# Gates of eight pairs loaded one token per partition, with a new order table and 123 fill-in matmuls

## The chip, the cores and the metric

The kernel runs on one NeuronCore of a Trainium2 chip. The core has a matrix engine (TensorE, PE in the profile, with its weight loads as PEld), a vector engine (VectorE, DVE), a scalar engine (ScalarE, ACT), a general engine (GpSimd, POOL) and a sync engine (SyncE, SP) that does nothing but start transfers. Transfers between the chip's memory and the core's on-chip memory run on 16 DMA engines, which all queues share. Each compute engine works through its own list of instructions in order; semaphores make it wait for others. The metric is the device time of one execution in microseconds, as the median of several runs.

## What is computed

The reference has two stages, all in float32. The inputs q, k, v and the gates a_re, a_im have the shape 4 x 8 x 768 x 48 (batch, head, token, feature).

The first stage is a recurrence over the tokens with a complex gate, in each batch and head:

```python
mag = np.sqrt(a_re * a_re + a_im * a_im)
scale = np.minimum(mag, 0.999) / (mag + 1e-06)
a_re_n, a_im_n = (a_re * scale, a_im * scale)
for t in range(S):
    new_re = ar * S_re - ai * S_im
    new_im = ar * S_im + ai * S_re
    S_re, S_im = (new_re + kv, new_im)        # kv: outer product of k[t], v[t]
    y[:, :, t] = np.einsum('bhd,bhde->bhe', q[:, :, t], S_re)
```

The second takes y as 4 x 768 rows of 384 features and applies a normalisation and an MLP with a residual:

```python
xn = (x - mu) / np.sqrt(var + 1e-06) * g_ln
ch = np.maximum(xn @ w_ch1, 0.0) @ w_ch2      # 384 -> 1536 -> 384
out = x + ch
```

## The kernel before

**Tiling.** The 768 tokens of a batch are six chunks of 128, taken two at a time: twelve pairs of chunks (P = 0 to 11, three per batch), 24 chunks (n = 0 to 23). Eight heads of 48 features lie side by side as 384 columns.

**From gates to a matrix product.** In logarithms the product of the gates up to a token is a cumulative sum. For each pair the kernel loads both gates (`are`, `aim`, 384 KB each, line 445), takes the log of the real part (`ln`), its inverse (`iv`), the ratio `r` = a_im / a_re, and from it the log magnitude (`r2`, `u`, `l`, `lc`) and the angle (`th`). Two groups of matmuls with a triangle of ones sum them over the tokens: `dec` (line 477, log magnitude) and `ph` (lines 492 to 496, angle in turns, with a carry `car` from the pair before). ACT then makes the decay `e`, its inverse `en`, and sine and cosine. q and k are multiplied by these (`qe`, `ke`, then `qs`, `ks`), transposed (`qT`, `kT` on PE with a copy out, or by a transposing DMA, line 599), and give a causal 128 x 128 score matrix per head (`am`, masked into `atm`). `gm` and `G` carry the state from chunk to chunk, `y` is the output of the recurrence, copied to `x`.

**The MLP.** x is transposed (`xtr`, `xT`), and each pair runs through 1536 hidden features in three groups: `mm1` (line 722), `relu` (lines 739 and 741, on ACT or DVE), `mm2` (line 754). Mean and scale of the normalisation are folded into the weights (`wp`, `wc`) and into the output scale `rstd`; `oa`, `ot` and `st` scale, add the residual and store (line 777).

**How tokens lie in the gate tiles.** For the gates alone partition p of a pair holds the two neighbouring tokens 2p and 2p + 1, so that one run in memory is 2 x 48 numbers, 384 B. q, k and v hold token p of each chunk, in runs of 192 B. The two cumulative sums turn the one arrangement into the other: for each of the two chunks c they add the products with two triangles `u_e[:, c, j]` (or `u_th`), j being the first or second token of a partition:

```python
for c in range(R):
    for j in range(R):
        nc.tensor.matmul(heads(ps[:, c]), lhsT=u_e[:, c, j], rhs=step(T("l", P), j),
                         start=(j == 0), stop=(j == R - 1))
```

That is four matmuls of 384 columns per pair and sum.

**The order of the work.** Nothing is scheduled on the chip. A table, `PLAN`, written out in full, holds all operations in one sequence, each with its engine (P, A, V, G, S for PE, ACT, DVE, POOL, SP) and, where it uses the accumulator memory, its bank. Every engine gets its operations in that sequence. For a load or a store the letter says which queue starts it, SP's or ACT's; a DMA that ACT starts stands in ACT's list with its arithmetic. `@name` makes an operation of POOL wait for the named one of DVE. Buffers are rings (line 26): three for the gates, q and k, two for v's load, four to five for what leaves.

**Fill-ins.** 134 matmuls without use (`warm`, line 787) stand among the work of the head and keep PE busy while the first gates are loaded and worked on.

Of the kernel before, what the change touches and what calls it, by code (L numbers as in the profile page):

```python
# [10 lines left out]
FP16 = mybir.dt.float16  # L11
# [23 lines left out]

ENGINES = {"P": "PE", "A": "ACT", "V": "DVE", "G": "POOL", "S": "SP"}
# [3 lines left out]
aim.0.0:A tab.log.0:A aim.0.1:A ue:G are.0.0:S are.0.1:S pad.e.1:G uth:V one:G warm.0:P0 pad.ks.0:G warm.1:P0  # L40
warm.2:P0 pick:G warm.3:P0 are.1.0:S warm.4:P0 warm.5:P0 warm.6:P0 k.0.1:S ln.0.0:A warm.7:P0 car0.1:G warm.8:P0
cmean:G iv.0.0:A warm.9:P0 ident:G warm.10:P0 warm.11:P0 r.0.0:V warm.12:P0 warm.13:P0 warm.14:P0 aim.1.0:S warm.15:P0
warm.16:P0 warm.17:P0 ln.0.1:A warm.18:P0 warm.19:P0 r2.0.0:A warm.20:P0 k.0.0:S warm.21:P0 warm.22:P0 warm.23:P0
warm.24:P0 u.0.0:A warm.25:P0 warm.26:P0 warm.27:P0 warm.28:P0 iv.0.1:A warm.29:P0 l.0.0:V warm.30:P0 are.2.0:S
warm.31:P0 warm.32:P0 ln.1.0:A warm.33:P0 warm.34:P0 r.0.1:G warm.35:P0 lc.0.0:V warm.36:P0 warm.37:P0 aim.2.0:S
warm.38:P0 warm.39:P0 warm.40:P0 iv.1.0:A warm.41:P0 warm.42:P0 pad.ks.1:G warm.43:P0 warm.44:P0 warm.45:P0 warm.46:P0
warm.47:P0 zdec:G r2.0.1:A warm.48:P0 pad.e.0:G warm.49:P0 pad.qs.0:G warm.50:P0 q.0.1:S warm.51:P0 warm.52:P0 u.0.1:A
warm.53:P0 warm.54:P0 r.1.0:V warm.55:P0 dec.0.0:P0 warm.56:P1 warm.57:P1 q.1.0:S e.0.0:A0 warm.58:P1 warm.59:P1
warm.60:P1 r2.1.0:V warm.61:P1 en.0.0:A0 warm.62:P1 warm.63:P1 warm.64:P1 l.0.1:V warm.65:P1 u.1.0:A warm.66:P1
warm.67:P1 warm.68:P1 warm.69:P1 lc.0.1:V warm.70:P1 are.3.0:S warm.71:P1 warm.72:P1 warm.73:P1 ln.2.0:A warm.74:P1  # L50
l.1.0:V warm.75:P1 warm.76:P1 warm.77:P1 warm.78:P1 dec.0.1:P6 q.1.1:S warm.79:P0 warm.80:P0 lc.1.0:V en.0.1:A6
warm.81:P0 warm.82:P0 warm.83:P0 warm.84:P0 q.0.0:S iv.2.0:A warm.85:P0 warm.86:P0 ke.0.1.0:G@lc.1.0 warm.87:P0
dec.1.0:P0 e.0.1:A6 r.2.0:V wl.1:G warm.88:P2 warm.89:P2 e.1.0:A0 warm.90:P2 warm.91:P2 warm.92:P2 warm.93:P2
warm.94:P2 gln:S r2.2.0:V en.1.0:A0 qrow:G dps.1:P4 dps.0:P5 ke.0.0.0:V warm.95:P2 warm.96:P2 u.2.0:A warm.97:P2
warm.98:P2 decc.1:V4 warm.99:P2 vf.0.0:S car0.0:G warm.100:P2 warm.101:P2 warm.102:P2 mask:G warm.103:P2 warm.104:P2
aim.3.0:S tab.trig.1:A warm.105:P2 warm.106:P2 warm.107:P2 wl.0:G qe.1.0.1:V warm.108:P2 warm.109:P2 vf.0.1:S
warm.110:P2 warm.111:P2 warm.112:P2 qe.1.0.0:V warm.113:P2 warm.114:P2 pad.qs.1:G warm.115:P2 warm.116:P2 l.2.0:V
th.0.0:A warm.117:P2 warm.118:P2 wl.2:G warm.119:P2 ph.0.0:P1 th.0.1:A th.1.0:A qe.0.0.0:V ph.0.1:P4 qe.0.1.0:V
warm.120:P0 warm.121:P0 warm.122:P0 k.1.0:S car.0.0:V1 decc.0:V5 sin.0.0:A1 lc.2.0:V sin.0.1:A4 qt.0.0:P1 ks.0.0.1:V
warm.123:P0 car.0.1:A4 wgc:V cos.0.0:A1 qt.0.1:P4 ph.1.0:P6 k.1.1:S ks.0.1.1:V cos.0.1:A4 qs.0.1.1:V th.2.0:A  # L60
# [153 lines left out]
def kernel(  # L214
# [14 lines left out]
    C = 128  # L229
# [594 lines left out]
```

## Time and profile before

| | us |
|---|---|
| median of 3 runs (lowest, highest) | 190.85 (190.52, 192.0) |
| the profiled execution | 192.75 |
| its span, first to last instruction | 191.0 |
| PE busy (2045 matmuls) | 177.3 |
| ACT busy | 158.9 |
| DVE busy | 156.6 |
| POOL busy | 105.5 |

The profile is of one execution. Busy time counts arithmetic: starting a transfer isn't counted, but while a queue engine does so it can do nothing else, and the profile shows such instructions as SPq and ACTq with a duration of their own. A matmul's duration is from its start to its modelled end; matmuls overlap, so the sum of durations is more than the time they take, and the chain of waits gives the step from one to the next. In the DMA rows a share of 1 means that the durations of all packets add up to 16 engines' time; packets overlap, so it can go above 1.

### The profile page before, as it was taken

The numbers are of one execution on the slowest core, as the hardware profiler recorded it, in microseconds if no ns is written. First come the engines' busy times: TensorE is split into PE (matmuls) and PEld (weight loads), VectorE is DVE, ScalarE is ACT, GpSimd is POOL, SyncE is SP. The second block draws the span as 40 slices with busy tenths as digits, with TensorE's granted clock in tenths as the row PEclk, the third lists the DMA queues.
The fourth block names the chain that finished last, engine by engine and source line by source line (L and its number), as shares of the span: only waits on it lengthen the run. The fifth ranks groups of instructions, "written<-read, shape, count | busy, mean of one in ns | idle before, by whom it ended". The sixth has DMA issues, their size and how long they took to land.

```text
span 191.0 us, 5154 instructions
## 1 busy us (share of the span) xinstructions
PE 177.3 (93%) x2045; PEld 138.6 (73%) x2045; DVE 156.6 (82%) x285; ACT 158.9 (83%) x224; POOL 105.5 (55%) x124
## 2 busy tenths in 40 slices
PE   5999398999999999999968999999999999998992
PEld 3888365788667887776847687877867777786781
DVE  1678699999999999999996998998989867666532
ACT  3989499999999997899949999998999979662340
POOL 7419032579196899071539483347785954940130
PEclk9999999999999999999999999999999999999998
DMA  6999999999969999889999999999799979994032
GB/s 153 278 240 202 212 198 204 210 214 207 242 108 287 205 220 234 154 183 234 136 265 234 190 221 230 282 223 204 141 160 262 217 126 179 256 191 151 5 124 82
DMA packets 133080, 37.57 MB, mean 197 GB/s; under 512 B 127168, under 2 KB 133056, under 8 KB 133056
## 3 DMA queue, kind: packets, MB, share of 16 engines
q1 hardware_dynamic: 107760, 27.21, 70.6%
q10 hardware_dynamic: 22512, 7.67, 18.0%
q0 software_dynamic: 2784, 2.36, 7.9%
q8 instruction: 16, 0.26, 0.6%
q14 instruction: 8, 0.07, 0.1%
HBM read 28.31 MB, written 4.72 MB: 173 GB/s over the span
## 4 chain that ended last, share of the span: by engine, by line
PE 63%; DVE 10%; ACT 9%; DMA 8%; issue 4%; ACTq 2%; POOL 1%; SPq 1%; DVEq 0%; POOLq 0%
PE banks L754 22%; PE banks L722 16%; PE banks L617 5%; PE banks L594 4%; DMA q<-in_q_dram 4%; DMA ksT<-ks 3%; PE banks L477 3%; PE banks L667 2%; ACTq L777 2%; PE banks L496 2%; PE banks L670 2%; DVE w1b L388 2%; DMA are<-in_a_re_dram 2%; PE banks L645 2%; PE banks L688 2%
## 5 line engine op out<-in xcount | busy, mean ns | idle before, releaser
L754 PE MATMUL banks<-w2b,h 128*128 128x384 bf16 (+1 forms) x300 | 55.7, 319 | 0.6 <-ACT h L739 0.6
L722 PE MATMUL banks<-xT,w1b 128*128 128x256 bf16 x432 | 50.9, 272 | 0.7 <-ACT h L739 0.5
L722 PEld LDWEIGHTS <-w1b 128*128 128x128 bf16 x432 | 41.4, 98 | 7.0 <-issue 1.2
L754 PEld LDWEIGHTS <-h 128*128 128x128 bf16 x300 | 26.7, 97 | 13.8 <-ACT h L739 1.0
L295 DVE TENSOR_TENSOR atm<-banks,mask 128x1024 bf16<-128x1024 f32 x24 | 29.0, 1219 | 3.8 <-PE banks L617 2.9
L739 ACT ACTIVATE h<-banks 128x1024 bf16<-128x1024 f32 (+1 forms) x26 | 25.7, 1009 | 4.6 <-DVE ks L295 2.6
L792 ACT ACT_TABLE_LOAD x19 | 24.4, 1283 | 2.6 <-PEq L808 1.3
L295 POOL TENSOR_TENSOR ke<-k,en 128x384 bf16<-128x384 f32 x17 | 15.4, 916 | 14.1 <-ACT e L481 4.3
L767 POOL TENSOR_TENSOR ot<-ot,x 128x384 f32<-128x384 f32 x13 | 12.5, 967 | 14.2 <-ACT ot L760 12.9
L295 POOL TENSOR_TENSOR r<-aim,are 128x768 f16<-128x768 f32 (+1 forms) x8 | 13.7, 1715 | 11.0 <-DVE w1b L388 4.1
L787 PE MATMUL banks<-u_e 128*128 128x256 f16 x134 | 17.5, 286 | 2.2 <-POOL u_e L323 2.2
L295 POOL TENSOR_TENSOR qs<-qe,trig 128x768 bf16<-128x768 bf16 x8 | 13.0, 1640 | 10.3 <-DVE w1b L388 7.2
L617 PE MATMUL banks<-qsT,ksT 128*128 128x128 bf16 x192 | 14.5, 219 | 2.8 <-ACT h L739 2.1
L787 PEld LDWEIGHTS <-u_e 128*128 128x128 f16 x134 | 13.5, 102 | 4.5 <-POOL u_e L323 1.9
L617 PEld LDWEIGHTS <-ksT 128*128 128x128 bf16 x192 | 12.1, 97 | 5.1 <-issue 2.8
L741 DVE TENSOR_SCALAR h<-banks 128x1024 bf16<-128x1024 f32 (+1 forms) x11 | 12.7, 1166 | 2.7 <-PE banks L722 2.7
L295 POOL TENSOR_TENSOR qe<-q,e 128x384 bf16<-128x384 f32 x12 | 11.0, 917 | 6.8 <-DVE r L295 3.6
L466 DVE SCALAR_TENSOR_TENSOR l<-r,w 128x768 f16<-128x768 f16 (+1 forms) x13 | 12.6, 969 | 1.3 <-ACT r L462 1.1
L680 DVE BATCH_NORM_STATS2 stats<-x 128x6 f32<-128x384 bf16 x24 | 13.1, 546 | 0.1
L667 PE MATMUL banks<-v,atm 128*128 128x48 bf16 x192 | 12.0, 183 | 0.0
L514 ACT ACTIVATE trig<-banks 128x768 bf16<-128x768 int16 (+1 forms) x13 | 9.8, 761 | 2.5 <-DVE car L509 2.4
L496 PE MATMUL banks<-th,u_th 128*128 128x384 f16 (+1 forms) x52 | 11.8, 313 | 0.0
(93 smaller groups left out, 380.8 us busy)
## 6 DMA issues: line engine op xcount, KB each, us to landing
k<-in_k_dram SPq DMA_DIRECT2D x24, 192.0 KB, 5.1
q<-in_q_dram SPq DMA_DIRECT2D x24, 192.0 KB, 4.3
are<-in_a_re_dram SPq DMA_DIRECT2D x11, 384.0 KB, 5.1
aim<-in_a_im_dram SPq DMA_DIRECT2D x11, 384.0 KB, 5.0
out_dram<-ot ACTq DMA_DIRECT2D x19, 192.0 KB, 3.4
vf<-in_v_dram ACTq DMA_DIRECT2D x18, 192.0 KB, 4.3
w1b<-in_moe_w_ch_dram POOLq DMA_DIRECT2D x3, 384.0 KB, 7.6
vf<-in_v_dram SPq DMA_DIRECT2D x6, 192.0 KB, 7.0
```

The source lines that it names most:

```text
L295: {"DVE": nc.vector, "POOL": nc.gpsimd}[eng(name)].tensor_tensor(**kw)
L466: nc.vector.scalar_tensor_tensor(out=S_("l"), in0=S_("r2"), scalar=0.5, in1=S_("w"), op0=ALU.mult, op1=ALU.add)
L496: nc.tensor.matmul(heads(ps[:, c]), lhsT=u_th[:, c, j], rhs=step(T("th", P), j), start=False, stop=(j == R - 1), skip_group_check=True)
L617: nc.tensor.matmul(ps[:, h], lhsT=T("ksT", n)[:, h], rhs=T("qsT", n)[:, h], start=True, stop=True)
L667: nc.tensor.matmul(ps[:, h], lhsT=T("atm", n)[:, h], rhs=T("v", P)[:, c, h], start=True, stop=nfirst)
L680: nc.vector.bn_stats(out=T("stats", n), in_=T("x", n))
L722: nc.tensor.matmul(ps[:, jj], lhsT=w1b[:, dc, ts(gi * JG + jj, C)], rhs=T("xT", P)[:, dc].rearrange("p c t -> p (c t)"), start=(dc == 0), ...
L739: act(out=dst, in_=src, func=AF.Relu)
L741: nc.vector.tensor_scalar(out=dst, in0=src, scalar1=0.0, scalar2=None, op0=ALU.max)
L754: nc.tensor.matmul(bank(own)[:, 0:w], lhsT=T("h", P)[:, j, ts(c, C)], rhs=w2b[:, j, es], start=(j == 0), stop=(j == NJ - 1))
L787: g.add(f"warm.{i}", lambda i=i: nc.tensor.matmul(bank(f"warm.{i}")[:, 0:256], lhsT=u_e[:, 0, 0], rhs=u_e[:, 1].rearrange("p j t -> p (j t ...
L792: g.add(f"tab.{nm}.{i}", lambda tab=tab: nc.scalar.preload_act_table_set(tab))
```

## The change

Three things change at once.

For the pairs 4 to 11 (`NATURAL`) the gates lie like q, k and v: token p of chunk c. Each gate is loaded as two transfers of 192 KB, one per chunk, in runs of 192 B (operations `are.P.0.c`, `aim.P.0.c`). The logarithms and the angle work on the same 768 columns as before. In the cumulative sums chunk 0 is one product with a triangle, and chunk 1 one with a block of ones (for chunk 0's tokens) and one with the triangle: three matmuls instead of four in `dec`, and three beside the two of the carry in `ph`. Two small tables, `n_e` and `n_th`, hold triangle and ones.

The order table is new from end to end, and its sequence of DMA issues is laid out for eight transfers under way at a time. Counted over both tables: SP starts 130 transfers (before 110) and ACT 38 (39). On ACT there are now 20 loads of q, k and the real gate's parts that SP started before, and 5 of v (18), 11 stores (19). Transposes by DMA: 13 of ks, 12 of qs, 3 of x (before 14, 11, 0). The arithmetic moves a little between engines; ACT, for one, has 1 square (4), 2 conversions of v (4), 15 copies of x (12), 27 ReLUs (26). POOL has 38 waits for its turn (27).

Fill-ins: 123 instead of 134. They stand in blocks of ten to forty, where the old table strewed them.

The code, without the table:

```diff
+NATURAL = {4, 5, 6, 7, 8, 9, 10, 11}
...
+    n_th = pool.tile([C, R, C], FP16, name="n_th")
+    n_e = pool.tile([C, R, C], FP16, name="n_e")
...
+    def c_ne():
+        nc.gpsimd.memset(n_e, 1.0)
+        nc.gpsimd.affine_select(out=n_e[:, 0], in_=n_e[:, 0], pattern=[[1, C]],
+                                compare_op=ALU.is_ge, fill=0.0, base=0, channel_multiplier=-1)
+
+    def c_nth():
+        nc.vector.tensor_scalar(out=n_th, in0=n_e, scalar1=INV2PI, scalar2=None, op0=ALU.mult)
...
-            def step(t, j, hs=hs):
+            nat = P in NATURAL
+
+            def step(t, j, hs=hs, nat=nat):
+                if nat:
+                    return t.rearrange("p h x -> p (h x)")[:, ds(j * DM, DM)].rearrange(
+                        "p (h d) -> p h d", d=D)
                 return t[:, hs].rearrange("p h (j d) -> p h j d", j=R)[:, :, j]
+
+            def sums(c, step_t, nat_t, nat=nat):
+                if nat:
+                    return [(nat_t[:, 0 if j == c else 1], j) for j in range(c + 1)]
+                return [(step_t[:, c, j], j) for j in range(R)]
...
+                if nat:
+                    for c in range(R):
+                        add(f"{nm}.{X}.{c}", lambda nm=nm, ap=ap, X=X, c=c, step=step: ring(
+                            f"{nm}.{X}.{c}").dma_start(out=step(T(nm, P), c), in_=ap[b].rearrange(
+                                "h (c p) d -> p c h d", p=C)[:, pp * R + c]), uses=[(nm, P)])
...
                 for c in range(R):
-                    for j in range(R):
-                        nc.tensor.matmul(heads(ps[:, c]), lhsT=u_e[:, c, j], rhs=step(T("l", P), j),
-                                         start=(j == 0), stop=(j == R - 1))
+                    parts = sums(c, u_e, n_e)
+                    for i, (lhsT, j) in enumerate(parts):
+                        nc.tensor.matmul(heads(ps[:, c]), lhsT=lhsT, rhs=step(T("l", P), j),
+                                         start=(i == 0), stop=(i == len(parts) - 1))
...
-                    for j in range(R):
-                        nc.tensor.matmul(heads(ps[:, c]), lhsT=u_th[:, c, j], rhs=step(T("th", P), j),
-                                         start=False, stop=(j == R - 1),
+                    parts = sums(c, u_th, n_th)
+                    for i, (lhsT, j) in enumerate(parts):
+                        nc.tensor.matmul(heads(ps[:, c]), lhsT=lhsT, rhs=step(T("th", P), j),
+                                         start=False, stop=(i == len(parts) - 1),
                                          skip_group_check=True)
...
-    for i in range(134):
+    for i in range(123):
```

The beginning and the end of the two tables, to show their kind:

```diff
-aim.0.0:A tab.log.0:A aim.0.1:A ue:G are.0.0:S are.0.1:S pad.e.1:G uth:V one:G warm.0:P0 pad.ks.0:G warm.1:P0
-warm.2:P0 pick:G warm.3:P0 are.1.0:S warm.4:P0 warm.5:P0 warm.6:P0 k.0.1:S ln.0.0:A warm.7:P0 car0.1:G warm.8:P0
...
-relu.11.2.0:V4 mm2.22.1:P6 mm2.23.1.0:P7 mm2.23.0.1:P0 mm2.23.1.1:P0 mm2.22.2:P6 ot.22:V6 mm2.23.2.0:P7 mm2.23.2.1:P0
-st.22:S ot.23.0:V7 st.23.0:S ot.23.1:V0 st.23.1:S
+ue:G cmean:G are.0.0:A tab.log.0:A ln.0.0:A zdec:G aim.0.0:S qrow:G iv.0.0:A r.0.0:V r2.0.0:G@r.0.0 are.1.0:S ln.1.0:A
+uth:V gln:S wgc:V u.0.0:A l.0.0:V lc.0.0:V warm.0:P0 warm.1:P0 warm.2:P0 warm.3:P0 warm.4:P0 warm.5:P0 warm.6:P0
...
+ot.22:V3 st.22:A st.20:S mm2.23.0.0:P7 mm2.23.1.0:P7 mm2.23.2.0:P7 ot.23.0:V7 mm2.23.0.1:P2 mm2.23.1.1:P2
+mm2.23.2.1:P2 ot.23.1:V2 st.23.0:S ot.19:G st.19:S st.23.1:A
```

More of the change, by code (lines that the diff above doesn't have):

```diff
@@ L44 @@
[L44 to L53, printed above, removed]
@@ L453, in pair_ops @@
                                                 op=ALU.mult),
-                needs=[f"iv.{X}", f"aim.{X}"], uses=[("are", P), ("aim", P), ("r", P)])
+                needs=[f"iv.{X}"] + ([f"aim.{X}.{c}" for c in range(R)] if nat else [f"aim.{X}"]), uses=[("are", P), ("aim", P), ("r", P)])
             def f_r2(S_=S_, X=X):
```

211 lines of the change are left out of this document (113 added, 98 removed).

## The prediction

> **What bounds the kernel now.** I read the busy times first, then stretches of ten microseconds, then the chain of waits, and last the groups, for prices.
>
> ```profile
> PE 177.3 (93%) x2045; PEld 138.6 (73%) x2045; DVE 156.6 (82%) x285; ACT 158.9 (83%) x224; POOL 105.5 (55%) x124
> ```
>
> TensorE (PE) is busy for 177.3 of 191.0 us. A total mixes stages, so here are the stretches; the columns are PE, PE weight load, DVE, ACT, POOL, granted clock, DMA share and GB/s.
>
> ```profile
> 60.00:70.00 10.00, 10.00 (x155) 8.47 (x154) 9.76 (x17) 9.69 (x16) 9.37 (x8) 1.00 1.05 223
> 70.00:80.00 10.00, 9.53 (x108) 8.05 (x106) 9.80 (x19) 8.56 (x11) 6.58 (x8) 1.00 0.88 203
> 90.00:100.00 10.00, 8.68 (x100) 6.91 (x96) 9.57 (x18) 7.35 (x11) 4.20 (x3) 1.00 1.12 193
> 120.00:130.00 10.00, 10.00 (x123) 8.22 (x122) 9.66 (x19) 9.62 (x14) 4.72 (x5) 1.00 1.15 259
> 170.00:180.00 10.00, 9.38 (x114) 6.94 (x113) 6.04 (x10) 3.38 (x6) 0.88 (x1) 1.00 0.35 109
> ```
>
> Two things are to be seen. PE is full (10.00 of 10) in good stretches like those from 60 and 120 and loses 0.47, 1.32 and 0.62 us in those from 70, 90 and 170: 2.4 us together. And ACT is hardly less full there: 9.69 and 9.62, without its DMA issues. The clock is at 1.00 where PE is full, so the fill-in matmuls do their work and there is nothing to win there.
>
> ```profile
> PE 63%; DVE 10%; ACT 9%; DMA 8%; issue 4%; ACTq 2%; POOL 1%; SPq 1%; DVEq 0%; POOLq 0%
> ```
>
> ```profile
> 13.77 7.08 DMA q<-in_q_dram
> ...
> 38.27 0.66 PE banks L722 x6
> ...
> 53.04 0.65 PE banks L477 x4
> ...
> 93.49 5.77 DMA ksT<-ks
> ...
> 131.75 0.34 PE banks L688 x6
> ```
>
> The chain that ended last is PE for 63%. The head, up to the first matmul of the MLP at 38.27, hangs on a load of q (7.08 us) and then on DVE; behind it the chain is nearly all PE, back to back. The piece at 93.49 is the exception: a DMA transpose of ks for which PE stood.
>
> So behind 38 us the rule is: work taken from PE comes off the end, as long as ACT and the loads keep step.
>
> **The change, part by part.** First the two cumulative sums per pair of chunks, lines 477 (log magnitude) and 496 (phase). The chain's steps give the price on a full PE, not the mean durations of the groups (here), which contain the overlapped fill of the array.
>
> ```profile
> L496 PE MATMUL banks<-th,u_th 128*128 128x384 f16 x44 | 10.7, 325 | 0.0
> ...
> L477 PE MATMUL banks<-l,u_e 128*128 128x384 f16 x44 | 8.9, 326 | 0.0
> ```
>
> Four matmuls of 384 columns take 0.65 us in the chain, so one takes 163 ns. With one token per partition chunk 0 doesn't depend on chunk 1: three products instead of four in each sum. Eight pairs, two sums, one product each: 16 x 0.163 = **-2.6 us** on PE, all of it behind the head. At the groups' 326 ns it would be 5.2 us; I keep that as the far end, but an instruction's overlap is not time that comes free.
>
> The new table sends more transposes through DMA: counted over both tables, three fewer of x (three matmuls each, 0.34 us for six, so 0.17), one fewer of qs and one more of ks (these two cancel). That is 3 x 0.17 = **-0.5 us** of PE.
>
> The 11 dropped fill-ins stand before the first MLP matmul, where PE waits for DVE and DMA; I cost them at **0**. What hides them is the head's chain; a fill-in is as wide as an MLP matmul (256 columns, 0.66 us for six), so without that cover they would be worth 11 x 0.11 = 1.2 us.
>
> Now the moved DMA issues. The instruction streams of ACT show what a held issue does:
>
> ```profile
> 70.37 2.37 ACTq L777 DMA_DIRECT2D out_dram<-ot  x1
> 70.98 0.84 ACT L485 ACTIVATE th<-r 128x768 f16<-128x768 f16 x1
> 72.77 1.28 ACT L792 ACT_TABLE_LOAD   x1 [0.95 <-issue]
> ```
>
> ```profile
> 170.83 2.45 ACTq L777 DMA_DIRECT2D out_dram<-ot  x3
> ...
> 173.33 0.20 ACT L704 ACTIVATE rstd<-mv 128x2 f32<-128x2 f32 x1 [1.53 <-DMA out_dram<-ot]
> ```
>
> A store's issue lasts 2.37 us there, and the table load behind it comes 0.95 us late; three stores late in the kernel make ACT wait 1.53 us before a ReLU that PE needs. These are the PE losses of 0.47 and 0.62 us above. The new table has 11 stores on ACT instead of 19, eight go to SP; in turn 20 loads of q, k and the gates come to ACT and 13 of v leave it (39 issues before, 38 after). Taking the two losses as gone gives **-1.1 us**; the bounds are -2.4 (all three stretches fill up) and, on the other side, +0.8: a load that ACT now issues can be held like that store, at 0.95 us, and two of them in a full stretch undo the gain and more.
>
> The Trainium skill (DMA: Bandwidth & Descriptors, "Issuing engines are not separate DMA queues") says that DMAs started by different engines run on the same 16 DMA engines and interleave. By that page the move between SP and ACT would win nothing but issue time, and the sum would end at -3.1; that ACT's store is held while SP's loads are under way agrees.
>
> What speaks against the change is the load of the gates. It was one transfer of 384 KB with runs of 384 B; it is two of 192 KB with runs of 192 B.
>
> ```profile
> k<-in_k_dram SPq DMA_DIRECT2D x24, 192.0 KB, 5.1
> q<-in_q_dram SPq DMA_DIRECT2D x24, 192.0 KB, 4.3
> are<-in_a_re_dram SPq DMA_DIRECT2D x11, 384.0 KB, 5.1
> ```
>
> k already comes in runs of 192 B, and half the bytes take the same 5.1 us: packets cost, not bytes. In two stretches, 5 to 10 us (mostly gates) and 150 to 155 us (one load of v on ACT's queue), the columns packets, MB and share are:
>
> ```profile
> q1 hardware_dynamic: 4677, 1.38, 110.7%
> ```
>
> ```profile
> q10 hardware_dynamic: 1040, 0.20, 20.5%
> ```
>
> v: 20.5% of 16 engines for 5 us is 16.4 us, over 1040 packets 15.8 ns for 192 B. Gates: 88.6 us over 4677, 18.9 ns at a mean of 295 B; as 384 B make up 54% of that, one such packet takes about 21.5 ns. A gate then costs 2048 x 15.8 = 32.4 us instead of 22.0: +10.4, and 16 gates +166 us, or 10.4 us on each of 16 engines. As a load on the path:
>
> ```profile
> DMA packets 133080, 37.57 MB, mean 197 GB/s; under 512 B 127168, under 2 KB 133056, under 8 KB 133056
> ```
>
> ```profile
> DMA packets 5504, 1.37 MB, mean 275 GB/s; under 512 B 5503, under 2 KB 5503, under 8 KB 5503
> ```
>
> Before: 133,080 packets in 191 us, 697 per us. After: 149,464 in some 187, 799 per us. The second row is 60 to 65 us: 1,101 per us went through there with PE full. So there is room on average, and I cost it at **0**: what hides it is that gates are loaded pairs ahead. If that cover goes, see the third rival.
>
> The other engines: by op counts DVE loses work and POOL gains about 7 us on its 105.5. Eleven more of POOL's instructions are made to wait for one of DVE (38 in the new table, 27 in the old); behind each stand POOL's next products ke, qe and the residual sums ot, which DVE, PE and the stores need. POOL idles for 85 us, and that hides both; I cost them at 0. ACT matters more, as it is nearly full:
>
> ```profile
> L739 ACT ACTIVATE h<-banks 128x1024 bf16<-128x1024 f32 x25 | 25.0, 1025 | 4.6 <-DVE ks L295 2.6 <-PE banks L722 1.8 <-issue 0.2
> ...
> L531 ACT ACTIVATE sh<-banks 128x768 f16<-128x768 int16 x8 | 6.5, 814 | 0.0
> L290 ACT CAST x<-banks 128x384 bf16<-128x384 f32 x12 | 5.7, 477 | 2.5 <-PE banks L670 2.5
> L290 ACT COPY xT<-banks 128x384 bf16<-128x384 bf16 x8 | 3.8, 481 | 5.2 <-PE banks L688 5.2
> L290 ACT CAST G<-banks 128x384 bf16<-128x384 f32 x8 | 3.8, 480 | 0.0
> L412 ACT CAST v<-vf 128x768 bf16<-128x768 f32 x4 | 3.3, 835 | 0.0
> ```
>
> Squares: two half and two full ones become a single full one; priced like the abs of the same 768 columns (0.81, a half at 0.5), -1.8. v: two fewer, -1.67. Abs: one fewer, -0.81. A G and an xT fewer, -0.96. ReLU one more, +1.03; the copy of ksT, as wide, one more, +1.03; x three more, +1.43; one short pair for rstd, at most a copy of x, +0.5. Sum about -1.3 us: ACT gets lighter, less than PE does.
>
> The new order of the head I cost at 0, with both signs open: up to the second xT, which releases the first MLP matmul, the sums over the tables come within a microsecond for ACT and DVE. Two more loads of k stand ahead of the last q, 2048 packets or 1.9 us at 1,101 per us; but the new DVE order puts q's product behind the phases that it held up before. Bounds: -2 and +1.9.
>
> **The sum.** -2.6 - 0.5 - 1.1 = -4.2 us. The profiled execution took 192.75 us, 1.75 more than its span of 191.0; its span would become 186.8. It lies 1.9 above the median of the runs shown, and I take the difference over to the median: 190.85 - 4.2 = **186.65 us**. A measurement here can't tell less than about 1% from no change, so 188.9 and 192.8 are the edges.
>
> **The rivals.**
> *ACT becomes the bound.* For it: 9.6 to 9.7 of 10 in the full stretches, with 38 issues to place besides. Against: 2.5 us of room in the stretches from 70 and 90, and it overlaps issues with running instructions. Then only ACT's own saving reaches the end: 190.85 - 1.3 = 189.55, no change that can be told. The head longer by its 1.9 with the rest as forecast gives 188.55, near the same edge.
>
> *The order does nothing for held issues* (the table allows for eight transfers under way, but the chip holds issues at another point). Then only the matmuls go: 190.85 - 3.1 = 187.75, still faster.
>
> *Loads come late, slower.* The place is SP's queue, where gate halves, q, k, v and the DMA transposes stand in one line:
>
> ```profile
> 20.76 6.93 SPq L404 DMA_DIRECT2D k<-in_k_dram  x2
> ```
>
> Two issues held SP for 6.93 us in the head. With 20 more issues on SP (110 to 130) and the extra packets, a transpose behind a held load comes late, and the piece at 93.49 shows the price: PE lost 1.32 us in that stretch. If it happens in n of the eight changed pairs, n x 1.32 stands against 3.1; from n = 3 the kernel is slower, and with five it is 190.85 - 3.1 + 6.6 = 194.35. For it: DMA shares of 1.12 and 1.15 now. Against: 60 to 65 us ran at 1,101 packets per us with no PE loss. The Trainium skill (same page, "Specifications") asks for runs of 512 B or more for full rate and puts a read-modify-write below that; by it this change goes the wrong way, though both sizes lie below its line. The trace agrees in direction: 15.8 ns for 192 B is 82 ns per 1000 B, 21.5 ns for 384 B is 56.
>
> **How the numbers follow.** Forecast, with its variants down to 184: 0.37; held issues unchanged, 187.75: 0.18; both are faster by over 1%, 0.55 together. ACT bound or a longer head, 188.9 to 192.8: 0.20. Late loads: 0.25. Eight times in ten between 184.0 (all three PE losses and 2 us of the head gone besides would be 183.4) and 195.0 (a little over five late pairs). The forecast's own range is 184 to 188.9.
>
> **What would show it.** Right: 16 fewer 384-column matmuls at the two lines of the sums, PE busy some 3 us less behind the head, no held store on ACT. Wrong: PE stretches below 9.5 between 45 and 165 us released by DMA or by the DMA transposes (late loads); PE idle ended by ReLU or trig on ACT at unchanged ACT sums (ACT bound); a first MLP matmul well off 38 us (head).

## The result, and the profile after

The changed kernel took 208.22 us in the median of four runs (205.07 to 211.03), the kernel before 190.78 in the same comparison. The ratio is 1.077, with a 95% interval of 1.064 to 1.090: 14.6 us slower (12.1 to 17.1; here and below a ratio is turned into us with 190.85). The forecast was 186.65 us, 4.2 us faster. The ratio leaves disturbed runs out, so it is smaller than that of the two medians, and the profiled execution shown here, 209.0 us with a span of 207.3, is one of the disturbed ones, so its clock is not read.

The page of the changed kernel, busy times and chain:

```profile
PE 181.4 (88%) x2009; PEld 140.1 (68%) x2009; DVE 163.2 (79%) x278; ACT 158.1 (76%) x223; POOL 114.2 (55%) x132
...
DMA  6999999999904999628999999999989998999113
...
PE 38%; DVE 25%; DMA 14%; ACT 11%; issue 5%; SPq 3%; POOL 2%; ACTq 1%; DVEq 0%; POOLq 0%
```

PE was 63% of the chain and is 38%; DVE went from 10% to 25%, DMA from 8% to 14%. DVE is busy for 6.6 us more than before (156.6), with seven instructions fewer. And the DMA engines, which stood at 9 tenths nearly throughout, fall to 0 and 4, and later to 6 and 2, in slices that lie between about 57 and 93 us.

The stretches that the prediction quoted (PE, PE weight load, DVE, ACT, POOL, clock, DMA share, GB/s):

```profile
60.00:70.00 10.00, 8.38 (x75) 5.54 (x75) 9.82 (x18) 7.12 (x10) 7.86 (x8) 0.83 0.49 91
70.00:80.00 10.00, 8.23 (x131) 6.67 (x128) 8.52 (x14) 6.79 (x12) 6.74 (x6) 1.00 1.06 228
90.00:100.00 10.00, 10.00 (x115) 7.40 (x114) 8.54 (x17) 9.91 (x15) 7.36 (x8) 1.00 0.74 148
120.00:130.00 10.00, 8.03 (x86) 6.34 (x84) 8.05 (x11) 6.26 (x9) 4.74 (x5) 1.00 1.11 200
170.00:180.00 10.00, 9.75 (x135) 7.95 (x133) 9.12 (x18) 6.87 (x10) 5.12 (x7) 1.00 1.16 180
```

Two of the three losses of before are gone or smaller (90 and 170), though at equal times the changed kernel is at earlier work than the kernel before. But 60 and 120, where PE was full, now lose 1.62 and 1.97 us, and 70 loses 1.77 instead of 0.47.

In the chain, the end of the head and what follows it:

```profile
31.36 0.58 DVE car L544
31.98 0.48 PE banks L556
...
43.54 0.66 PE banks L757 x6
...
54.82 1.67 DVE l L499
56.49 1.92 DVE ke L299
```

The first product of the MLP starts at 43.54 instead of 38.27. Behind it the chain, which was PE back to back, stands on DVE, and single DVE operations are long.

The groups of the two sums show that the products were dropped as counted: 24 products with the new triangle and block of ones in each sum, where 32 were.

```profile
L531 PE MATMUL banks<-th,n_th 128*128 128x384 f16 x24 | 6.5, 326 | 0.0
...
L511 PE MATMUL banks<-l,n_e 128*128 128x384 f16 x24 | 5.7, 349 | 2.9 <-DVE l L502 2.9
```

### The profile page after: what moved, and what is told of

It reads as the page before. It is cut to its first block, busy times and chain, and to the rows that moved or that the text cites. A ratio compares the mean times of both kernels' runs of the same rounds, so it can differ in the third digit from the quotient of the medians.

```text
span 207.3 us, 5107 instructions
## 1 busy us (share of the span) xinstructions
PE 181.4 (88%) x2009; PEld 140.1 (68%) x2009; DVE 163.2 (79%) x278; ACT 158.1 (76%) x223; POOL 114.2 (55%) x132
## 4 chain that ended last, share of the span: by engine, by line
PE 38%; DVE 25%; DMA 14%; ACT 11%; issue 5%; SPq 3%; POOL 2%; ACTq 1%; DVEq 0%; POOLq 0%
PE banks L789 12%; PE banks L757 10%; DMA are<-in_a_re_dram 7%; DMA qsT<-qs 5%; PE banks L652 3%; DVE qs L299 3%; PE banks L629 3%; DMA xT<-x 3%; DVE ks L299 2%; DVE atm L299 2%; DVE l L499 2%; DVE ke L299 2%; DVE h L776 2%; DVE r L299 2%; DVE stats L715 2%
## 5 line engine op out<-in xcount | busy, mean ns | idle before, releaser
L757 PE MATMUL banks<-xT,w1b 128*128 128x256 bf16 x432 | 53.5, 277 | 3.5 <-DMA xT<-x 1.9
L757 PEld LDWEIGHTS <-w1b 128*128 128x128 bf16 x432 | 41.7, 99 | 10.5 <-DMA xT<-x 2.5
L789 PEld LDWEIGHTS <-h 128*128 128x128 bf16 x300 | 27.6, 99 | 13.7 <-issue 1.6
L299 POOL TENSOR_TENSOR r<-aim,are 128x768 f16<-128x768 f32 x8 | 14.5, 1812 | 18.9 <-ACT are L483 13.2
L299 POOL TENSOR_TENSOR qe<-q,e 128x384 bf16<-128x384 f32 x15 | 14.3, 963 | 11.0 <-DMA q<-in_q_dram 7.9
L802 POOL TENSOR_TENSOR ot<-ot,x 128x384 f32<-128x384 f32 x13 | 12.1, 935 | 14.6 <-ACT ot L795 12.2
L299 POOL TENSOR_TENSOR ke<-k,en 128x384 bf16<-128x384 f32 x15 | 14.3, 953 | 10.1 <-DMA k<-in_k_dram 4.7
L776 DVE TENSOR_SCALAR h<-banks 128x1024 bf16<-128x1024 f32 x10 | 12.2, 1220 | 4.8 <-PE banks L757 4.7
L299 POOL TENSOR_TENSOR ks<-ke,trig 128x768 bf16<-128x768 bf16 (+1 forms) x8 | 12.4, 1549 | 5.2 <-ACT trig L549 4.5
L299 DVE TENSOR_TENSOR qs<-qe,trig 128x768 bf16<-128x768 bf16 (+1 forms) x20 | 13.6, 693 | 0.5 <-POOL qe L299 0.3
L702 PEld LDWEIGHTS <-atm 128*128 128x128 bf16 x192 | 11.1, 97 | 4.0 <-issue 2.3
L430 POOL TENSOR_SCALAR v<-vf 128x768 bf16<-128x768 f32 x8 | 6.7, 840 | 12.5 <-DMA vf<-in_v_dram 8.5
```

The costliest lines, as they stand in the source:

```text
L299: {"DVE": nc.vector, "POOL": nc.gpsimd}[eng(name)].tensor_tensor(**kw)
L702: nc.tensor.matmul(ps[:, h], lhsT=T("atm", n)[:, h], rhs=T("v", P)[:, c, h], start=True, stop=nfirst)
L757: nc.tensor.matmul(ps[:, jj], lhsT=w1b[:, dc, ts(gi * JG + jj, C)], rhs=T("xT", P)[:, dc].rearrange("p c t -> p (c t)"), start=(dc == 0), ...
L776: nc.vector.tensor_scalar(out=dst, in0=src, scalar1=0.0, scalar2=None, op0=ALU.max)
L789: nc.tensor.matmul(bank(own)[:, 0:w], lhsT=T("h", P)[:, j, ts(c, C)], rhs=w2b[:, j, es], start=(j == 0), stop=(j == NJ - 1))
L802: nc.gpsimd.tensor_tensor(out=T("ot", n)[:, es], in0=T("ot", n)[:, es], in1=T("x", n)[:, es], op=ALU.add)
```

## The experiments

The change has two halves that can be run alone: how the gates lie and are summed, and the table.

**Each half alone.** The old table with the new gates, every gate's load written as two at its old place:

```diff
-are.4.0:S
+are.4.0.0:S are.4.0.1:S
```

> The order table and the 134 fill-ins of before, with the gates of pairs 4 to 11 loaded one token per partition (each gate load replaced in place by its two halves). It tells the gates from the table. If the table is what costs (theory A), this is no slower than before: PE has 16 products of 0.163 us less, 188 us, and at most 193 with 16 more transfers in the rotation. If the new gate loads are what costs (theory B: 16,384 more packets, loads late), it lies near the changed kernel, above 200 us.

And the new table with `NATURAL = set()`, each gate loaded once, where the first of its two loads stood:

```diff
-NATURAL = {4, 5, 6, 7, 8, 9, 10, 11}
+NATURAL = set()
```

> The new order table and 123 fill-ins, with the gates of all pairs loaded as before (two tokens per partition, one transfer of 384 KB at the place of the first half). The counterpart of the run above. Theory A (the table costs): 203 to 212 us, as the changed kernel or up to 3 us more for the 16 products. Theory B (the gate loads cost): near 192.

Measured: 199.06 us for the gates (ratio 1.044, 1.037 to 1.051: +8.4 us) and 202.46 us for the table (1.062, 1.056 to 1.068: +11.8 us). Each half costs by itself; together they cost less than their sum of 20.2. So there are two causes to find.

In the first of the two traces ACT stands behind its own transfers:

```profile
133.49 0.49 ACT L295 CAST x<-banks 128x384 bf16<-128x384 f32 x1
136.13 0.38 ACTq L813 DMA_DIRECT2D out_dram<-ot  x1
136.60 0.48 ACT L295 CAST x<-banks 128x384 bf16<-128x384 f32 x1 [2.63 <-DMA q<-in_q_dram]
```

A store that ACT issues waits until a load of q, started by SP, has landed; the copy that PE needs waits behind it for 2.63 us. The semaphores that the trace records say why: the 165 transfers that SP and ACT start in this run take eight semaphores in turn, over both queues, and none of the 157 that follow another on its semaphore starts before that one, the eighth before it in the order of the table, has landed. This store has the semaphore of the load of q that SP started at 130.04. So there are three suspects in this half: 16,384 more pieces, 16 more transfers in the rotation of eight, and ACT's own issues.

**The gates taken apart.** All four runs have the old table; in the first two the outputs of the changed pairs are not the reference's. First only the sums, on old loads:

```diff
-                    return [(step_t[:, c, j], j) for j in range(R)]
+                    if nat:
+                        return [(nat_t[:, 0 if j == c else 1], j) for j in range(c + 1)]
```

> The old order table and the old loads (two tokens per partition, 384-byte pieces, one transfer per gate), and only the sums of the last eight pairs are cut from four products to three, as with one token per partition. The outputs of those pairs are then not the reference's: the sums run over the tokens in the wrong order. It prices the gain by itself. Theory 'the sums are worth what the prediction said, and the loads eat it': 188.1 us (2.6 us below 190.7). Rival 'behind the head something else than TensorE binds, so a shorter TensorE gives nothing': 190.7 us, no change.

Then the sums with all the pieces, in as many transfers as before (taken from other places in memory):

```diff
+    out=T(nm, P).rearrange("p h x -> p (h x)").rearrange("p (g d) -> p g d", d=D),
+    in_=ap[b].rearrange("h s d -> (h s) d").rearrange(
+        "(g p) d -> p g d", p=C)[:, pp * R * H:(pp + 1) * R * H]
```

> The old order table, the sums of three products, and every gate of the last eight pairs in ONE transfer of 2,048 pieces of 192 bytes, taken from sixteen blocks of tokens that follow each other in memory (so the gates' values are those of other tokens, and those outputs are not the reference's). Beside the old-table run with the new gates (199.1 us) it has the same pieces and sixteen fewer transfers. Theory P 'the 16,384 extra pieces load the DMA engines, which were nearly full already (the rows of the profile before: 97% of the 16 engines' span), and everything that waits for a landing waits longer': about 199 us, as with two transfers. Theory R 'the sixteen extra transfers use up the eight that may be outstanding, and hold issues': 188 to 191 us.

The transfers without the pieces:

```diff
+    hh = ds(c * (H // R), H // R)
+    out=T(nm, P)[:, hh], in_=ap[b][hh].rearrange("h (k p j) d -> p k h (j d)", p=C, j=R)[:, pp]
```

> The old order table, the old sums (four products) and the old pieces of 384 bytes, but every gate of the last eight pairs in two transfers of four heads each: sixteen more transfers than before, no more pieces. The outputs are the reference's. Theory P 'the pieces cost': 190.7 to 192 us. Theory R 'the transfers cost': about 199 to 201 us. If both share in it: in between, and what it has over 190.7 is the share of the transfers.

And the new gates with ACT's 37 later issues on SP (as in the first line, for each):

```diff
-vf.3.0:A
+vf.3.0:S
```

> The old order table with the new gates (199.1 us), and every DMA that ScalarE issued after the first two (18 loads of v, 19 stores) is issued by SyncE at the same place of the table. Theory H 'the lost time reaches TensorE through ScalarE, whose own DMA issues wait for the landing of the eighth transfer before them, with its evictions behind them (2.63 us ahead of the copy at 136.60 us of that run)': 190 to 194 us. Theory L 'the loads come late whoever issues them': 199 us or, since SyncE then waits for the stores' data as well, up to 205 us.

| old table, and | us | ratio (95%) | against before, us |
|---|---|---|---|
| three products a sum | 190.76 | 0.997 (0.994 to 1.001) | -0.5 |
| the same and the pieces | 198.29 | 1.029 (1.021 to 1.037) | +5.5 |
| two transfers a gate, old pieces | 191.47 | 1.004 (1.001 to 1.008) | +0.8 |
| new gates, no issues on ACT | 197.37 | 1.036 (1.029 to 1.043) | +6.8 |
| new gates whole (from above) | 199.06 | 1.044 (1.037 to 1.051) | +8.4 |

The first and the third are too small to be called a change. Theory P holds: the pieces cost 6.0 us (5.5 + 0.5; by the two intervals some 4 to 8), the extra transfers 0.8 alone. With the pieces and two transfers together another 2.9 appear (8.4 - 5.5; the two intervals only just miss each other), of which taking the issues off ACT gets 1.6 back; there the intervals, 1.036 against 1.044, overlap, so that this last share is not shown. The pieces are seen in the queue rows (packets, MB, share of 16 engines' span), first of the sums alone, span 188.6 us, then with the pieces, span 194.2 us:

```profile
q1 hardware_dynamic: 107760, 27.21, 71.5%
q10 hardware_dynamic: 22512, 7.67, 16.9%
```

```profile
q1 hardware_dynamic: 124144, 27.21, 76.0%
q10 hardware_dynamic: 22512, 7.67, 16.7%
```

The same bytes. 88.4% of 188.6 us is 166.7 us on each engine, 92.7% of 194.2 is 180.0: 13.3 us more. In that run the kernel became 6.0 us longer for them, so a good half was hidden.

The run of the sums alone has a second message. In its chain PE is 48% and DVE 23%, against 63% and 10%. PE's work shrank (175.7 us busy, 177.3 before) and the end hardly moved. That DVE became late in PE's place is a reading of this one chain and not shown: in the run with two transfers a gate, which drops no product, the chain has PE at 50% as well.

**The table in two parts.** Up to the first product of the MLP both tables list nearly the same operations, so their first parts can be exchanged there; what is then left stands in the order of the other table. All gates are the old ones.

```diff
-ue:G cmean:G are.0.0:A tab.log.0:A ln.0.0:A zdec:G aim.0.0:S
...
+aim.0.0:A tab.log.0:A aim.0.1:A ue:G are.0.0:S are.0.1:S
...
 mm1.0.0.0:P0 relu.0.0:A0 G.2:A7 atm.3:V4 mm1.0.1.0:P2
```

> Old gates everywhere. The order table of the kernel before up to the first product of the MLP (320 entries, all 134 fill-ins), and from there the order of the changed table. With the old gates the whole changed table took 202.5 us, 11.8 us more than before. Theory T 'the first part of the table costs what its first MLP product is late (42.50 us against 38.10 us in the two traces, 4.4 us), the rest costs the other 7.4 us': 198 us. Rival 'all of it lies in the first part, and the later gaps follow from a head that lags': 190.7 to 192 us. Rival 'the head's lag is absorbed later': 202 us.

> Old gates everywhere. The changed table up to the first product of the MLP (with its 123 fill-ins), and from there the order of the table before: the counterpart of the run above. Theory T: 195 us (4.4 us above 190.7). Rival 'all of it lies in the first part': 202 us. Rival 'the head's lag is absorbed later': 190.7 to 192 us.

Old first part and new rest: 201.02 us (1.040, 1.025 to 1.054: +7.6, from 4.8 to 10.3). New first part and old rest: 196.17 us (1.023, 1.014 to 1.032: +4.4, from 2.6 to 6.1). They add up to 12.0, against 11.8 for the whole. Theory T's sizes hold: the first part costs some 4.4 us, and the rest some 7.6 us by itself, without the late head. In the second run the first product of the MLP starts at 43.51 us, 5.4 later than before (38.10); whether this lateness is all of the 4.4 us is not shown.

In the first of these two traces, DVE, POOL and PE in the stretch from 50 us, and a stretch of 2.5 us behind it (PE busy, clock, DMA share, GB/s):

```profile
50.73 1.67 DVE L498 SCALAR_TENSOR_TENSOR l<-r,w 128x768 f16<-128x768 f16 x1
52.32 1.99 DVE L298 TENSOR_TENSOR ke<-k,en 128x384 bf16<-128x384 f32 x1
```

```profile
50.50 1.09 POOL L298 TENSOR_TENSOR qe<-q,e 128x384 bf16<-128x384 f32 x1 [3.74 <-DVE l L498]
51.66 2.23 POOL L298 TENSOR_TENSOR qs<-qe,trig 128x768 bf16<-128x768 bf16 x1
```

```profile
57.34 1.12 PE L510 MATMUL banks<-l,u_e 128*128 128x384 f16 x4 [3.00 <-DVE l L501]
```

```profile
57.50:60.00 2.50, 2.50 (x17) 0.54 0.00 0
```

POOL works on qe and qs at that time, DVE's l and ke take 1.67 and 1.99 us (0.95 and 0.55 when POOL stands, see below), PE stands 3.00 us for the clip that comes behind them, and the clock is at 0.54 after that. The DMA engines are empty meanwhile (0.00). In the new first part the same picture, at 27 us:

```profile
27.45 2.37 DVE L297 TENSOR_TENSOR ks<-ke,trig 128x384 bf16<-128x384 bf16 x1
...
31.24 0.56 DVE L542 TENSOR_SCALAR car<-banks 32x384 f16<-32x384 int16 x1
```

```profile
27.95 1.65 POOL L297 TENSOR_TENSOR qs<-qe,trig 128x768 bf16<-128x768 bf16 x1
```

```profile
31.85 0.48 PE L554 MATMUL banks<-qrow,pick 128*128 128x384 f16 x1 [2.74 <-DVE car L542]
```

```profile
30.00:32.50 2.50, 0.65 (x2) 0.66 1.20 213
32.50:35.00 2.50, 2.50 (x18) 0.50 1.28 241
35.00:37.50 2.50, 2.50 (x14) 0.50 1.28 228
```

Two possible causes are in these rows: empty DMA engines, and DVE and POOL side by side.

**Empty DMA engines.** In the changed kernel SP stood 15.6 us for a transpose of qs, with all its later loads behind it (us in total, times, longest):

```profile
SPq L634 <- DVE qs L299: 18.6, 3, 15.6
```

Three runs go at this. In the changed kernel 52 loads of SP go ahead of the transposes and stores before them; one of them:

```diff
-qsT.6:S ... vf.3.1:S
+vf.3.1:S qsT.6:S
```

> The changed kernel with 52 loads on SP's queue moved ahead of the group of DMA transposes and stores that stands right before them; nothing else moves. Theory C: loads are late because SP waits in order for a transpose's source (15.6 us once, with the DMA engines idle meanwhile). Then the hole in the DMA row from 55 to 66 us is filled and the time falls by 4 to 10 us, to 198 to 204. If the order of DVE and POOL is what makes everything late, with the loads only following, less than 2 us.

And the one transpose done by PE, in the changed kernel and in the changed table with old gates:

```diff
-qsT.6:S ... kT.6:P2 ... ksT.6:V2
+qT.6:P3 kT.6:P2 ... qsT.6:V3 ksT.6:V2
```

> The changed kernel, but the transposes of q of token tile 6, for which SyncE stood 15.6 us with every later load behind it, is done by TensorE (eight transposes, about 1.05 us) and evicted by VectorE (0.68 us), so that SyncE issues the loads behind it at once. Theory E 'the DMA engines are nearly full all the time, so what they do not move in the hole (busy share 0.83 and 0.49 in 50 to 70 us, against 1.06 around it: some 8 us of their work) comes late afterwards and is lost': 200 to 202 us. Rival 'the loads in the hole are not needed until much later': 208 us, or 209 us with the added transposes.

> The same edit in the changed table with the old gates (202.5 us), where SyncE stood 24.9 us at that place and the DMA engines' busy share was 0.61 and 0.59 in 50 to 70 us (some 9 us of their work). Theory E: 194 to 196 us. Rival 'not needed until later': 202.5 us or 1 us more.

Moving the loads made it worse, 214.97 us (1.126, 1.120 to 1.133), and the hole stayed: the DMA share from 60 to 70 us was 0.45 instead of 0.49. Now transposes stand behind loads: from 118.50 on SP needs six us for four loads, then come two transposes, and PE stands 8.66 us for them.

```profile
118.50 2.46 SPq L420 DMA_DIRECT2D q<-in_q_dram  x1
...
124.50 4.07 SPq L634 DMA_TRANSPOSE qsT<-qs  x2
```

```profile
130.18 1.03 PE L652 MATMUL banks<-qsT,ksT 128*128 128x128 bf16 x8 [8.66 <-DMA qsT<-qs]
```

The transpose on PE gave 205.73 us (1.073, 1.064 to 1.083; the changed kernel 1.077), the same within the error, and with the old gates 203.4 to 207.9 us, no better than the 201.3 to 203.2 without it. But these two did not do what they were made for: SP went a few loads on and then stood for a store, 13.4 us in the changed kernel, and the DMA engines were as empty as before, only a little later.

```profile
SPq L812 <- DVE ot L805: 16.0, 2, 13.4
```

```profile
60.00:70.00 10.00, 8.49 (x76) 5.63 (x76) 9.82 (x19) 7.08 (x10) 7.86 (x8) 0.83 0.20 39
```

So none of the three runs filled the hole and theory E was not tested; it stays open what the empty engines cost. What SP stands for, both times, is a product or an output of DVE.

**More fill-ins.** The changed kernel with 108 more, ahead of five stands of PE (24, 26, 20, 20 and 18):

```diff
-dec.4.0:P4
+warm.147:P4 ... warm.172:P4 dec.4.0:P4
```

> The changed kernel with 108 more fill-ins, put in front of the five matmuls before which PE idled for 1.9 to 2.9 us (11.9 us together, 108 x 0.11 us). If the halved clock after these gaps costs time of its own (theory D), the mean granted clock goes from 0.96 to 0.99 or more and the time falls by 3 to 6 us, to 202 to 205. If PE waits for others anyway, the clock rises and the time stays within 2 us of 207, or grows by up to the fill-ins' own 12 us where the gaps moved.

205.56 us, ratio 1.077 (1.070 to 1.085), the ratio that it has without them, at a mean clock of 0.98 to 1.00 in its four runs: by that, the 3 to 6 us of theory D are not there; a smaller share could hide in the intervals. The first 24 stand in the head. There the clock from 30 to 37.5 us is 1.00 instead of 0.50 to 0.57, PE's stand for the carry `car` falls from 2.74 to 0.3 us, and the first product of the MLP starts 2.1 us earlier (41.31 instead of 43.38 in the two timelines). At the end nothing of these 2.1 us is to be seen, though the intervals are wide enough to hide them.

**DVE and POOL side by side.** Four runs let POOL wait at one place of each part until DVE is through; every engine's order stays.

```diff
-qs.1.0.1:G ... qe.2.0.1:G@l.3.0 ... qs.2.0.0:G
+qs.1.0.1:G@car.1.0 ... qe.2.0.1:G@lc.4.0 ... qs.2.0.0:G@lc.4.0
```

> The changed table's first part with the rest of the old table and the old gates (196.2 us), and one wait more: GpSimd's product qs of pair 1 (1.65 us, at 27.95) starts only when VectorE has written the carry of pair 1. In the trace without the wait VectorE's 128x384 product ks beside it took 2.37 us, where such a one takes 0.35 us in the kernel before; the carry followed at 31.24, TensorE stood 2.74 us for it, and its clock was halved in the next ten us. Theory C 'the two engines slow each other down, and the operations that the late one waits for pay': the 2.7 us stand falls below 1 us, the halved clock goes, the time is 193 to 194.5 us. Rival O 'VectorE's order is late, whatever GpSimd does': 196 us or, with the later GpSimd product, 197 us.

> The old table's first part with the rest of the changed table and the old gates (201.0 us), and two waits: GpSimd's products qe (second half) and qs (first half) of pair 2 start only when VectorE has done the clip of pair 4. Without them, in 50 to 57 us, VectorE's product ke took 1.99 us, l 1.67, ks 1.16 and the clip 0.65 us, where such ones took 0.66, 0.95, 0.56 and 0.36 us elsewhere in that trace or in the kernel before, some 2.9 us more, and TensorE stood 3.00 us for the clip. Theory C: the stand goes below 0.8 us, 196 to 198.5 us. Rival O: 201 us or more.

> The whole changed table with the old gates (202.5 us) and the three waits of the two runs above. Theory C, with both parts: 196 to 198.5 us. Rival O: 202 us or more.

> The changed kernel (208.2 us) and the three waits. Theory C: 201.5 to 204.5 us, what is left being the pieces of the gates and the late stores and loads. Rival O: 208 us or more.

| | without | with the waits | ratio without | ratio with (95%) |
|---|---|---|---|---|
| new first part | 196.17 | 197.03 | 1.023 | 1.025 (1.020 to 1.031) |
| new rest | 201.02 | 202.79 | 1.040 | 1.051 (1.045 to 1.057) |
| new table, old gates | 202.46 | 205.91 | 1.062 | 1.073 (1.067 to 1.079) |
| changed kernel | 208.22 | 208.13 | 1.077 | 1.089 (1.082 to 1.095) |

Theory C is right on the spot, and the time did not fall. The new first part with the wait, DVE, then POOL, then PE:

```profile
27.36 0.35 DVE L297 TENSOR_TENSOR ks<-ke,trig 128x384 bf16<-128x384 bf16 x1
...
33.54 3.82 DVE L297 TENSOR_TENSOR qs<-qe,trig 128x768 bf16<-128x768 bf16 x1
```

```profile
33.08 1.64 POOL L297 TENSOR_TENSOR ks<-ke,trig 128x768 bf16<-128x768 bf16 x1
34.66 0.53 POOL L370 MEMSET ks<- 128x512 bf16 x1
35.14 1.80 POOL L297 TENSOR_TENSOR r<-aim,are 128x768 f16<-128x768 f32 x1
```

```profile
29.73 0.32 PE L554 MATMUL banks<-qrow,pick 128*128 128x384 f16 x1 [0.72 <-DVE car L542]
...
37.51 0.66 PE L627 MATMUL banks<-ident,qs 128*128 128x128 bf16 x8 [3.49 <-DVE qs L297]
```

Without a product of POOL beside it DVE's product takes 0.35 us again instead of 2.37, and PE's stand shrinks from 2.74 to 0.72. But POOL's next products now fall beside DVE's next one, which takes 3.82 us, and PE stands 3.49 us for that. In the new rest it is the same: l and ke are back at 0.95 and 0.55 us,

```profile
50.82 0.95 DVE L498 SCALAR_TENSOR_TENSOR l<-r,w 128x768 f16<-128x768 f16 x1
51.69 0.55 DVE L298 TENSOR_TENSOR ke<-k,en 128x384 bf16<-128x384 f32 x1
...
55.63 3.17 DVE L298 TENSOR_TENSOR qe<-q,e 128x384 bf16<-128x384 f32 x2
```

and two products of qe pay 3.17 us in their place. The Trainium skill (SBUF — State Buffer, "SBUF: two separate sides") says that GpSimd and some of VectorE's instructions, among them those with two inputs in SBUF against a GpSimd instruction that reads SBUF, hold a common pair of ports one at a time, each for a whole instruction, and that the other is blocked meanwhile. The rows agree for the products: the 3.82 us end 0.42 us after POOL's third instruction.

The last two runs undo the sharing-out. In the new first part eight products go back to the engine that they had before; in the new rest 47 products and casts:

```diff
-qe.0.1.0:G ... qs.0.1.0:G
+qe.0.1.0:V ... qs.0.1.0:V
```

> The changed table's first part with the rest of the old table and the old gates (196.2 us), with eight products of the first part on the engine that they had before: six from GpSimd to VectorE, two from VectorE to GpSimd. Theory C2 'the sharing-out costs: six products of 0.9 to 1.65 us beside VectorE's stretch those': first product of the MLP 2 to 4 us earlier than its 43.5 us, 192.5 to 194.5 us. Rival O 'the order of the first part costs': 196 us or more, as VectorE has more to do in it.

> The old table's first part with the rest of the changed table and the old gates (201.0 us), with the 47 products and casts of that rest that the changed table puts on the other of VectorE and GpSimd back where they were. Theory C2: 195 to 198 us. Rival O: 200 us or more, since an order written for one sharing-out does not suit another.

198.08 us (1.035, 1.027 to 1.042) against 196.17, and 218.90 us (1.126, 1.116 to 1.136) against 201.02. C2 falls: the old sharing-out in the new order is clearly slower in the rest and not faster in the first part. The new sharing-out in the old order was not run.

What these six runs did to the stretching can be added up from the traces: for each instruction of DVE the time beyond the median of its kind (operation, tiles and shape, over all runs), where that is more than 0.1 us. In the changed kernel these are 20 instructions, each beside an instruction of POOL.

| | DVE beyond the medians, us | time against before, us |
|---|---|---|
| before | 4.5 | 0 |
| new first part; with the wait; with the old sharing-out | 8.0; 9.6; 8.1 | 4.4; 4.8; 6.6 |
| new rest; with the waits; with the old sharing-out | 10.5; 10.4; 18.8 | 7.6; 9.7; 24.0 |
| new table, old gates; with the waits | 13.8; 15.1 | 11.8; 14.0 |
| changed kernel; with the waits | 13.8; 15.3 | 14.6; 16.9 |

So none of the runs took the stretching away: the waits moved it, and in the rest the old sharing-out made more of it. Stretching and time go together. That makes it the likely way by which the table costs, but no run lowered it alone, so it is not shown.

**What is settled.** The gates: some 6.0 us from the pieces, some 2.9 more with two transfers of such pieces, and nothing that can be told from zero won by the sums (0.5). The table: some 4.4 us in its first part and 7.6 behind it. **What stays open:** which decision of the table costs these, and what the empty DMA engines cost. In the traces DVE is late there, its products beside POOL's take up to seven times as long, and the DMA engines run empty while SP waits for DVE; moving the waits moved the losses. No run here beat the kernel before by more than its error.

## Why the prediction was wrong, point by point

*"Work taken from PE comes off the end, as long as ACT and the loads keep step."* This step failed first. Alone, the 16 dropped products were worth 0.5 us (from 1.1 gained to 0.2 lost), not 2.6. The step in the chain was read rightly; but the chain is the one path that ended last, and the work behind it did not move up with it. Which path held it is not shown. DVE is the likely one: the rows quoted had it at 9.76 and 9.80 of 10 in the stretches from 60 and 70, and I checked ACT's room and not DVE's.

*Packets at 0.* This is the largest wrong term of the gates. The load was sized well, 10.4 us on each of 16 engines against 13.3 measured. What I let hide it was wrong: I took one stretch of five us at 1,101 packets per us as the capacity and the average of 697 as the use. The rows beside it had DMA shares of 1.05, 1.12 and 1.15, and the queue rows of the page before, which I had not quoted, add up, with two small queues not shown here, to 97% of the 16 engines' span:

```profile
q1 hardware_dynamic: 107760, 27.21, 70.6%
q10 hardware_dynamic: 22512, 7.67, 18.0%
q0 software_dynamic: 2784, 2.36, 7.9%
```

A share near 1 is no hard limit here (packets overlap), but the room was not there to be counted on: 6.0 us of the load came through.

*Held issues, -1.1.* Failed as far as the traces show; no run has the moved issues alone. The term counted the losses from 70 and 170 as gone. The one from 170 is small now, but the one from 70 grew from 0.47 to 1.77 us, and all of it came by the same path: ACT's issues are held until the eighth transfer before them has landed, whoever started it (in the changed kernel none of 160 starts earlier). ACT and then PE there:

```profile
78.26 0.43 ACTq L474 DMA_DIRECT2D are<-in_a_re_dram  x1
78.80 0.81 ACT L549 ACTIVATE trig<-banks 128x768 bf16<-128x768 int16 x1 [2.28 <-DMA are<-in_a_re_dram]
```

```profile
80.36 0.37 PE L680 MATMUL banks<-v,ks 128*128 128x48 bf16 x8 [2.13 <-ACT sh L566]
```

The load that ACT issues at 78.26 has the semaphore of one that SP started at 72.82. Such an issue holds what stands behind it in ACT's list and not what is already running: in the prediction's rows the arithmetic of 70.98 ran beside the issue of 70.37, and only the table load behind it was late. A changed mix of 38 issues does not get rid of that. What the prediction put against this term from the Trainium skill (DMA: Bandwidth & Descriptors, "Issuing engines are not separate DMA queues") was the better guide here: the issues moved and the holds stayed.

*The order of the head, 0, from -2 to +1.9.* Measured +4.4 (2.6 to 6.1), outside both bounds. I summed work per engine and found it equal; but the new order lets POOL's products run beside DVE's, and DVE took longer there: 8.0 us beyond the medians in that run against 4.5 before. For the order behind the head the sum has no term at all: it was put at nothing without a reason, and with 7.6 us (4.8 to 10.3) it is the largest miss.

*POOL's 7 us more and its 11 waits, 0, "POOL idles for 85 us".* POOL's idle time was no cover, because the price falls on DVE. Its busy time rose by 6.6 us with fewer instructions, where I had it lose work: in the changed kernel its instructions took 13.8 us beyond the medians, against 4.5 before.

*Transposes of x by DMA, -0.5.* No run has them alone. In the changed kernel one of the three made PE wait 1.9 us, nearly four times the sum that I had put down for all; with the transpose of qs on PE it was 1.06.

*Fill-ins, 0.* Nothing speaks against it: 108 more, 24 of them in the head, did not help at the end. *ACT, -1.3:* it lost 0.8 us of busy time (158.9 to 158.1), in a kernel that DVE held up more than ACT.

*The rivals.* "Loads come late" had the right sign and the right object, the runs of 192 bytes. The rule beside it from the Trainium skill (DMA: Bandwidth & Descriptors, "Specifications") pointed the same way, and the 13.3 us of engine time agree in direction; no run here shows the read-modify-write itself. Its price was wrong in kind: it counted late transposes at 1.32 us in so many pairs, 194.35 us with five of them, while the engines' time for the pieces was the quantity to use. The piece from which that price came was also misread: in the kernel before PE did not stand for the transpose at 93.49 but for a ReLU of ACT, behind a store whose issue had the transpose's semaphore and so waited for its landing, the same hold as above (ACT, then PE):

```profile
99.28 0.36 ACTq L777 DMA_DIRECT2D out_dram<-ot  x1
```

```profile
100.81 0.61 PE L617 MATMUL banks<-qsT,ksT 128*128 128x128 bf16 x8 [2.13 <-ACT h L739]
```

No rival had DVE, and none had the table as a cost beyond a head longer by 1.9 us.

*What was to show it.* Sixteen fewer products: yes. PE busy 3 us less: not in the profiled execution (181.4 against 177.3); in the run of the sums alone it was 1.6 less, 175.7. Stretches below 9.5 between 45 and 165 us: yes, but the largest was released by DVE, which the list did not have. First product of the MLP off 38 us: yes, 43.54.

## What to carry to other kernels

Where PE, ACT, DVE and the DMA engines are all nine tenths busy in the same stretch, as here, work taken off one of them can be worth little (0.5 of 2.6 us) and work put on another can come through in good part (6.0 of 13.3): before an extra is put down at nothing, read the busy share of what has to carry it, in the stretches where it falls. Price runs of a load in engine time per piece, not in bytes, and hold it against the share of the DMA engines that is left. A new order of many operations is a change with a price of its own, in which a sum of work per engine says nothing about who runs beside whom; measure it apart from what it comes with.

## What was not expected of the hardware

A DVE product of 128x384 took 2.37 us instead of 0.35 beside a memset and a product of POOL, and one of 128x768 took 3.82 us beside three POOL instructions in a row: DVE did not get in between them. DVE's instructions that read the accumulator banks kept their time: in the changed kernel all 24 products with the mask (`atm` from `banks`) took 1.21 to 1.23 us, 21 of them beside work of POOL. All 20 that were stretched had their operands in tiles, none in `banks`.

Transfers of SP and ACT wait for one another through the eight semaphores they share (in three traces none of 458 starts before the eighth before it has landed): ACT's arithmetic stood 2.63 us for a load of q that SP had started.

After a PE stand of 2.74 us the granted clock was 0.50 for the five us that followed, and after one of 3.00 us 0.54 in the next 2.5; the kernel before had a stand of 2.62 us at 22.93 without such a loss.
